# Gate and up of a decode block with stationary weights, and shorter norms

## The chip, the cores and the metric

The kernel runs on 1 core of one Trainium2 chip. The metric is device time in microseconds (us), as the median of several executions. The engines of the core that matter here are PE (TensorE: matmuls, and PEld, the loads of their stationary weights), DVE (VectorE), ACT (ScalarE), POOL (GpSimd) and SP (SyncE, whose queue issues all data transfers here). Each engine works through its own instructions in order; semaphores order them between engines.

## The reference, cut to what matters

```python
def _A_ref(x, k_cache, v_cache, wq, wo):
    q = (x @ wq).reshape(B, Sq, Hq, Dh).transpose(0, 2, 1, 3)
    k = jnp.repeat(k_cache, rep, axis=1)
    v = jnp.repeat(v_cache, rep, axis=1)
    scores = jnp.einsum("bhqd,bhkd->bhqk", q, k) * (Dh ** -0.5)
    o = jnp.einsum("bhqk,bhkd->bhqd", _softmax(scores), v)
    return o.transpose(0, 2, 1, 3).reshape(B, Sq, Hq * Dh) @ wo

def _B_ref(x, w_gate, w_up, w_down):
    h = _sigmoid(x @ w_gate) * (x @ w_up)
    return h @ w_down

x = x + _A_ref(_layernorm(x), A_k_cache, A_v_cache, A_wq, A_wo)
x = x + _B_ref(_layernorm(x), B_w_gate, B_w_up, B_w_down)
x = x + _A_ref(_layernorm(x), A_k_cache, A_v_cache, A_wq, A_wo)
x = x + _B_ref(_layernorm(x), B_w_gate, B_w_up, B_w_down)
```

Four batch rows, one token each, width 512, 32 query heads, 8 heads of keys and values with 4096 positions of 128 values, inner width 1792 (14 blocks of 128). All inputs are bfloat16. The two attention layers read the same caches.

## The kernel before, in words

One head of one batch row has 1 MB of keys and 1 MB of values. The kernel holds 12 slots of 1 MB each. `seq` lists all (layer, batch row, head) in the order worked out by hand in `ORDER`, which interleaves layer 1 of finished batch rows with layer 0 of the others; two heads make a group, 32 groups in all. Part of the slots (`RET`) are kept from layer 0 to layer 1, so that 52 MB of values and 48 MB of keys are loaded instead of 64 each.

The loop over `plan` (L1218) has 33 steps. Step k works on the softmax of group k (`sg`) and on the values of group k - 1 (`vg`), and prepares the keys of group k + 1 (`nxt`). In order, a step issues: the second scores of `sg` (L943), the sums of `vg` (L1017), `q_blocks` (POOL, L680), the first `k_turn` (a transpose of a slot on DVE, L928), `smax` (DVE, L966 and L970), one output projection `wo_pair` (L1130, with the addition to the residual x, L1144), `spread_max` (L977), `softmax` (L986 on DVE, L994 on ACT), `inverse` (L1027), the second `k_turn`, `pv` of the two heads (L1079), `normalise` (L1112), `ptrans` (L1039 on PE, 16 copies L1062 on ACT). The first scores of the next group come where `FIRST_AT` says. Since each engine keeps this order, whatever stands ahead of an instruction in its queue delays it.

`pump` (L383) issues the transfers in the fixed order of `loads`, built from the table `LOADS` (L327 to L363): it issues as long as a slot is free. A slot comes free when the scores that read the keys, or the pv that reads the values, are done; the queue on SP waits for that.

Between the two layers each batch row goes through a pass: norm, gate and up, down, norm, q. It is cut into 19 steps (`pass_steps`, L894), and `PLACES` (L57) says for every one at which point (0 to 8) of which loop step it is issued, relative to the step that ends the row's layer 0. The four passes run, by the profile, at about 92 to 114 us (row 0), 148 to 171 us (row 1), 205 to 229 us (row 2) and 262 to 285 us (row 3).

A pass works as follows. `ln_a` (L502): a matmul with ones sums x (L508), DVE takes the sum (L513), subtracts the mean (L520, float32 `xc`), ACT copies this to bfloat16 (`xc_bf`, L528), DVE squares it (L533). `ln_b_sum` sums the squares on PE (L585); `ln_b_rs` takes the sum (L593), divides and adds eps (L600), makes a first guess of the reciprocal root by integer arithmetic (L605) and refines it in three Newton steps of two instructions (L542, L550). The norm's factor `rs` is not applied to the operand but to what comes out of the matmuls. `gate_row` (L737) holds one column of `xc_bf` as weights and moves gate's weights, 512 or 384 columns at a time, 16 matmuls in all; each result is one row of PSUM, in four strips of partitions. `gate_tanh` (L754) makes half of rs (L756) and takes the tanh over 512 columns (L761). `up_row` (L766) is like gate. `up_gate` copies up's rows on ACT (L784) and multiplies on DVE (L786). `h_turn` turns the rows into 14 columns by 4 matmuls (L797) and copies them out (L803). `down` (L858) has stationary weights: 56 matmuls with a 128x128 block each and one moving column (L863). `down_add` adds to x in two instructions (L876, L886). Then come the second norm, `q_row`, `q_out`, `q_turn` and `q_spread`.

At the end all four rows go together through norm, `gate_up` (L690, stationary weights, four moving columns, L696) and `down_rows` (L1328), and the result leaves by one transfer.

Of the kernel before, what the change touches and what calls it, by code (L numbers as in the profile page):

```python
# [5 lines left out]
dt = mybir.dt  # L6
# [195 lines left out]
def bass_interleave_layers__gqa_block_cached__glu_gated_glu__decode_kernel(  # L202
# [17 lines left out]
    P = 128  # L220
# [12 lines left out]
    RSQRT_MAGIC = float(0x5F375A86)  # L233
    exp_scale = float(DH) ** -0.5
    RS = -1.0 / 8192.0
# [24 lines left out]
    rsg = small[:, 2:3]  # L260
# [14 lines left out]
    sq_sb = sbt([P, KD, Bn], dt.float32, "sq")  # L275
    dn_sb = sq_sb
    newt = sbt([P, 9, Bn], dt.float32, "newt")
    lnsum, lnsq, vpe, nt_a, nt_b, nt_c, nt_y, rs = [newt[:, i, :] for i in range(8)]
# [66 lines left out]
    need("k", 0)  # L345
    need("k", 1)
    for k, (_, vg) in enumerate(plan):
        sg = plan[k + 1][0] if k + 1 < len(plan) else None
        at = {"k": sg, "v": vg}
        got = {"k": 0, "v": 0}  # L350
        for o in range(2):
            for kind in LOADS[k][2 * o:2 * o + 2]:
                if at[kind] is not None:
                    need(kind, 2 * at[kind] + got[kind])
                got[kind] += 1
            if 2 <= 2 * k + o < 2 + HKV:
# [4 lines left out]
        assert got == {"k": 2, "v": 2}  # L361
# [140 lines left out]
    def ln_a(b0, nb):  # L502
# [15 lines left out]
        )  # L518
        dve(
            lambda e: e.scalar_tensor_tensor(  # L520
                out=xc_sb[:, :, 0:nb], in0=bc(lnsum[:, 0:nb], KD, nb), scalar=-inv_d, in1=xs,
                op0=ALU.mult, op1=ALU.add,
            ),
            reads=xkeys + ["lnsum"],
            writes=["xc"],
        )
        act(
            lambda e: e.activation(xc_bf[:, :, 0:nb], xc_sb[:, :, 0:nb], ACTF.Copy),  # L528
            reads=["xc"],
            writes=["xcb"],  # L530
        )
        dve(
            lambda e: e.tensor_tensor(sq_sb[:, :, 0:nb], xc_sb[:, :, 0:nb], xc_sb[:, :, 0:nb], ALU.mult),  # L533
# [4 lines left out]
    def newton_one(y0):  # L538
        y, yk = y0, "y0i"
        for it, three in enumerate((3.0, 12.0, 768.0)):  # L540
# [17 lines left out]
    def newton_many(y0, nb):  # L558
        y, yk = y0, "y0i"
        for it, three in enumerate((3.0, 12.0, 768.0)):  # L560
# [19 lines left out]

    def ln_b_sum(nb):
# [3 lines left out]
            lambda e: e.matmul(M[:, 32:32 + KD * nb], lhsT=ones_w, rhs=sq_sb[:, :, 0:nb], start=True, stop=True),  # L585
# [4 lines left out]
    def ln_b_rs(nb):  # L590
# [3 lines left out]
                lnsq[:, 0:nb], M[:, 32:32 + KD * nb].rearrange("p (k b) -> p b k", k=KD), AX.X, ALU.add  # L594
            ),
            reads=["M1"],
            writes=["lnsq"],
# [92 lines left out]
    def gate_up(nb, which, h=None):  # L690
# [14 lines left out]
        if which == 0:  # L705
# [11 lines left out]
                lambda e: e.activation(t_sb[:, 0:KF * nb], gs_sb[:, 0:KF * nb], ACTF.Tanh, scale=0.5 * RS),  # L717
# [689 lines left out]
```

## Time and profile before

| | us |
|---|---|
| median of 3 executions | 320.65 (319.68 to 321.61) |
| the profiled execution | 324.28 |
| its span, first to last instruction | 322.1 |
| PE busy, of the span | 221.3 |
| DVE busy | 183.6 |
| ACT busy | 139.6 |
| transfers (DMA): read from memory | 118.76 MB, 369 GB/s over the span |

The views used below: the page's first line and busy times; the chain of work that ended last; the busy time by stretch, whose columns are the stretch, its length, then for PE, PEld, DVE, ACT and POOL the busy time and (in brackets) the instructions, then PE's granted clock as a share, the share of the DMA engines and GB/s; the chain in order of time (start, duration, what); the timeline (start, duration, engine, line, operation, output<-inputs, shapes, how many; in square brackets the idle time ahead and what ended it); groups by line and shape (busy us, mean ns of one | idle time before and what ended it).

### The profile page before, as it was taken

The numbers are of one execution on the slowest core, as the hardware profiler recorded it, in microseconds if no ns is written. First come the engines' busy times: TensorE is split into PE (matmuls) and PEld (weight loads), VectorE is DVE, ScalarE is ACT, GpSimd is POOL, SyncE is SP. The second block draws the span as 40 slices with busy tenths as digits, with TensorE's granted clock in tenths as the row PEclk, the third lists the DMA queues.
The fourth block names the chain that finished last, engine by engine and source line by source line (L and its number), as shares of the span: only waits on it lengthen the run. The fifth ranks groups of instructions, "written<-read, shape, count | busy, mean of one in ns | idle before, by whom it ended". The sixth has DMA issues, their size and how long they took to land.

```text
span 322.1 us, 11493 instructions
## 1 busy us (share of the span) xinstructions
PE 221.3 (69%) x4892; PEld 154.8 (48%) x4892; DVE 183.6 (57%) x473; ACT 139.6 (43%) x602; POOL 25.8 (8%) x106
## 2 busy tenths in 40 slices
PE   1435413133278998868898787699885989988785
PEld 0423312122156565655656555555553665566675
DVE  4477343240656529965542898464776567469244
ACT  1005221204045257644615675452564753377530
POOL 0000000000000010110001001000100000020200
PEclk9999999999999555555755555575555555565555
DMA  7999999999999999998799999999999999999700
GB/s 293 428 422 408 403 404 402 401 387 388 401 415 367 360 382 424 419 419 326 245 368 355 425 422 418 419 388 378 371 421 421 421 418 404 391 371 424 322 3 5
DMA packets 22255, 119.50 MB, mean 371 GB/s; under 512 B 1976, under 2 KB 7868, under 8 KB 8892
## 3 DMA queue, kind: packets, MB, share of 16 engines
q1 hardware_dynamic: 22204, 118.77, 92.6%
q8 instruction: 39, 0.64, 0.8%
q14 instruction: 12, 0.10, 0.1%
HBM read 118.76 MB, written 0.00 MB: 369 GB/s over the span
## 4 chain that ended last, share of the span: by engine, by line
PE 33%; DMA 33%; DVE 16%; SPq 12%; issue 4%; ACT 1%; POOL 1%; DVEq 0%
DMA slot<-in_A_v_cache_dram 24%; PE O_ps L1079 9%; DVE slot L928 9%; PE S_ps L943 8%; SPq L403 6%; DMA wo<-in_A_wo_dram 5%; SPq L389 5%; PE M_ps L814 4%; DMA slot<-in_A_k_cache_dram 3%; PE O_ps L1130 3%; PE M_ps L508 2%; PE M_ps L863 2%; PE MS L977 2%; DVE small L966 1%; PE M_ps L696 1%
## 5 line engine op out<-in xcount | busy, mean ns | idle before, releaser
L1062 ACT ACTIVATE pT<-PT 32x64 bf16<-32x64 f32 x496 | 106.7, 215 | 67.1 <-PE PT L1039 54.1
L928 DVE STREAM_TRANSPOSE slot<-slot 128x2048 f32<-128x2048 f32 (+1 forms) x61 | 112.0, 1837 | 40.2 <-DMA slot<-in_A_k_cache_dram 40.2
L1079 PE MATMUL O_ps<-pT,slot 128*128 128x4 bf16 x1984 | 61.3, 167 | 29.4 <-DMA slot<-in_A_v_cache_dram 26.6
L1079 PEld LDWEIGHTS O_ps<-pT,slot 128*128 128x128 bf16 x1984 | 59.5, 104 | 36.1 <-DMA slot<-in_A_v_cache_dram 27.5
L943 PE MATMUL S_ps<-slot,qz 128*32 128x256 bf16 x1024 | 65.5, 409 | 14.7 <-DVE slot L928 11.2
L943 PEld LDWEIGHTS S_ps<-slot,qz 128*32 128x32 bf16 x1024 | 30.7, 128 | 32.1 <-DVE slot L928 13.0
L994 ACT ACTIVATE pe<-S_ps,small 128x256 bf16<-128x256 f32 x32 | 15.1, 473 | 50.0 <-issue 31.2
L1008 POOL TENSOR_TENSOR small<-small 128x1 f32<-128x1 f32 x64 | 12.4, 193 | 244.8 <-ACT pe L994 242.3
L977 PE MATMUL MS<-ident_bf,small 128*128 128x128 bf16 x64 | 12.5, 300 | 23.9 <-DVE small L970 23.6
L1130 PE MATMUL O_ps<-oT,wo 128*128 128x2 bf16 (+1 forms) x640 | 20.8, 165 | 4.9 <-issue 3.8
L1130 PEld LDWEIGHTS O_ps<-oT,wo 128*128 128x128 bf16 x640 | 19.1, 104 | 6.7 <-issue 4.6
L977 PEld LDWEIGHTS MS<-ident_bf,small 128*128 128x128 bf16 x64 | 4.2, 109 | 33.0 <-DVE small L970 26.3
L1112 DVE TENSOR_TENSOR oT<-O_ps,rden 128x8 bf16<-128x8 f32 x32 | 5.4, 168 | 24.9 <-PE O_ps L1079 24.7
L966 DVE TENSOR_REDUCE small<-S_ps 128x1 f32<-128x256 f32 x32 | 12.7, 397 | 12.0 <-PE S_ps L943 12.0
L680 POOL TENSOR_TENSOR qz<-qc,small 128x128 bf16<-128x128 bf16 x32 | 12.6, 399 | 35.4 <-ACT qc L666 35.4
L986 DVE CUSTOM_DVE_ANT_0 junk<-MS,mask_f,small 128x128 bf16<-128x128 f32 x32 | 10.7, 336 | 7.4 <-PE MS L977 7.2
L814 PE MATMUL M_ps<-wq,xc_bf 128*1 128x512 bf16 x128 | 14.5, 625 | 0.0
L1039 PE MATMUL PT<-ident_bf,pe 128*128 128x128 bf16 x64 | 11.7, 283 | 1.4 <-ACT pe L994 1.4
L666 ACT ACTIVATE qc<-M_ps 128x128 bf16<-128x128 f32 x8 | 1.9, 280 | 22.7 <-PE M_ps L655 22.7
L1017 PEld LDWEIGHTS MS<-head_b,small 128*128 128x128 bf16 x96 | 5.0, 107 | 12.7 <-issue 12.7
L1144 DVE TENSOR_TENSOR xT<-xT,O_ps 128x4 f32<-128x4 f32 x32 | 4.0, 157 | 12.0 <-PE O_ps L1130 11.8
L761 ACT ACTIVATE M_ps<-M_ps,small 128x512 f32<-128x512 f32 x4 | 2.6, 662 | 14.5 <-DVE small L756 14.5
(93 smaller groups left out, 171.9 us busy)
## 6 DMA issues: line engine op xcount, KB each, us to landing
slot<-in_A_v_cache_dram SPq DMA_DIRECT2D x52, 1024.0 KB, 11.4
slot<-in_A_k_cache_dram SPq DMA_DIRECT2D x48, 1024.0 KB, 10.8
wq<-in_A_wq_dram SPq DMA_DIRECT2D x4, 1024.0 KB, 7.6
wo<-in_A_wo_dram SPq DMA_DIRECT2D x8, 512.0 KB, 16.1
wg<-in_B_w_gate_dram SPq DMA_DIRECT2D x4, 448.0 KB, 13.8
wu<-in_B_w_up_dram SPq DMA_DIRECT2D x4, 448.0 KB, 14.2
wd<-in_B_w_down_dram SPq DMA_DIRECT2D x2, 896.0 KB, 16.5
row<-in_A_x_dram SPq DMA_DIRECT2D x1, 4.0 KB
```

Of the source, the lines that this page charges most:

```text
L389: S.dma("sp", (lambda dst, src: lambda e: e.dma_start(dst, src))(dst, src), f"wo{n}" if kind == "wo" else kind, writes=[f"{kind}{n}"])
L403: S.dma("sp", (lambda dst, src: lambda e: e.dma_start(dst, src))(dst, src), f"d{s}", writes=[f"s{s}"])
L680: lambda e: e.tensor_tensor(qz_sb[z][:, :, 0:4 * REP].rearrange("p i (a r) -> p i a r", r=REP), qc_sb[:, b, u:u + 2, :, :].rearrange("p u ...
L814: (lambda k, st: lambda e: e.matmul(M_ps[h][32 * st:32 * st + 1, :], lhsT=xc_bf[:, k, 0:1], rhs=wv[:, k, h, :, st, :], start=(k == 0), sto ...
L928: dve(lambda e: e.transpose(kf, kf), writes=[f"s{st}"])
L943: (lambda t, b2, e_, w0, s: lambda e: e.matmul(S_ps[p][32 * s:32 * s + 8 * REP, 0:2 * P], lhsT=qzf[:, w0:w0 + 8 * REP], rhs=ktv[:, :, s, : ...
L966: lambda e: e.tensor_reduce(m, S_ps[p][:, 0:2 * P], AX.X, ALU.max),
L977: (lambda n, col: lambda e: e.matmul(MS[:, 0:P], lhsT=top(col).broadcast_to([P, P]), rhs=ident_bf[:, :], start=(n == 0), stop=(n == 1)))(n ...
L994: lambda e: e.activation(pe_sb[p].rearrange("p j m -> p (j m)"), S_ps[p][:, 0:2 * P], ACTF.Exp, bias=nm_sb[p], scale=exp_scale, accum_out= ...
L1062: (lambda dst, frm: lambda e: e.activation(dst, frm, ACTF.Copy))(dst, frm),
L1079: (lambda x, c, j: lambda e: e.matmul(O_ps[p][:, ul * REP:(ul + 1) * REP], lhsT=vv[:, x * JG + c * 2 + j, :], rhs=pT[:, x, j, 2 * c + ul, ...
L1130: (lambda c, r: lambda e: e.matmul(O_ps[p][:, 64 + 2 * c:64 + 2 * c + nb], lhsT=wo_sb[:, u * REP + r, c * P:(c + 1) * P], rhs=oT_sb[n][:, ...
```

## The change

- `LOADS` is read in another way (one running count of keys and one of values, instead of counts within a step), with its first and last entries rewritten. A table `STEP` says for every step where the first `k_turn` stands, whether the first pv comes early, and whether the second `k_turn` is made in two halves; this last was a condition.
- In the passes gate and up become `wide`: 56 matmuls each, with a 128x128 block of the weights stationary and one moving column, into 14 columns of PSUM. `up_gate` and `h_turn` go; one DVE instruction, `gate_mul`, multiplies (tanh - 1) with up, straight into the columns that `down` reads. `PLACES` loses one entry for each row.
- In the norms DVE writes the bfloat16 operand itself, ahead of the float32 one. The squares get a fifth block that holds eps, so that the sum brings it along, and the division is folded into the constants of the Newton steps.
- A scale `RS` of -2 instead of -1/8192 saves the halving of rs. `down_add` is one instruction. The residual addition of a `wo_pair` with two rows is one instruction instead of two.

```diff
-    "kvkv", "kvkv", "kvkv", "vkkv", "kvkv", "kvkv", "kvkv", "vkvk",
+    "kkkk", "kvkv", "kvkv", "vkkv", "kvkv", "kvkv", "kvkv", "vkvk",
...
-    "vkkv", "kvkv", "kvkv", "kvkv", "kvkv", "kvkv", "kvkv", "kvkv",
-    "kvkv",
+    "vkkv", "kvkv", "kvkv", "kvkv", "kvkv", "kvkv", "kvkv", "vv",
+    "vv",
+)
+
+
+STEP = (
+    0, 0, 0, 0, 0, 0, 0, 6,
+    6, 6, 6, 6, 0, 6, 6, 6,
+    6, 6, 6, 0, 6, 6, 6, 6,
+    6, 6, 0, 0, 6, 6, 6, 0,
+    0,
 )
...
-    need("k", 0)
-    need("k", 1)
-    for k, (_, vg) in enumerate(plan):
-        sg = plan[k + 1][0] if k + 1 < len(plan) else None
-        at = {"k": sg, "v": vg}
-        got = {"k": 0, "v": 0}
+    got = {"k": 0, "v": 0}
+    for k, kinds in enumerate(LOADS):
         for o in range(2):
-            for kind in LOADS[k][2 * o:2 * o + 2]:
-                if at[kind] is not None:
-                    need(kind, 2 * at[kind] + got[kind])
+            for kind in (kinds[:2], kinds[2:])[o]:
+                need(kind, got[kind])
                 got[kind] += 1
...
-        act(
-            lambda e: e.activation(xc_bf[:, :, 0:nb], xc_sb[:, :, 0:nb], ACTF.Copy),
-            reads=["xc"],
-            writes=["xcb"],
-        )
+        for out, key in ((xc_bf, "xcb"), (xc_sb, "xc")):
+            dve(
+                (lambda out: lambda e: e.scalar_tensor_tensor(
+                    out=out[:, :, 0:nb], in0=bc(lnsum[:, 0:nb], KD, nb), scalar=-inv_d, in1=xs,
+                    op0=ALU.mult, op1=ALU.add,
+                ))(out),
+                reads=xkeys + ["lnsum"],
+                writes=[key],
+            )
...
-            lambda e: e.matmul(M[:, 32:32 + KD * nb], lhsT=ones_w, rhs=sq_sb[:, :, 0:nb], start=True, stop=True),
+            lambda e: e.matmul(M[:, 32:32 + (KD + 1) * nb], lhsT=ones_w, rhs=sq_sb[:, :, 0:nb], start=True, stop=True),
...
-        dve(
-            lambda e: e.tensor_scalar(vpe[:, 0:nb], lnsq[:, 0:nb], inv_d, eps, op0=ALU.mult, op1=ALU.add),
-            reads=["lnsq"],
             writes=["vpe"],
...
+    def wide(which):
+        wsb, keys = ((wg_sb, wkeys["wg"]), (wu_sb, wkeys["wu"]))[which]
+        fns = []
+        for fc in range(KF):
+            for k in range(KD):
+                fns.append(
+                    (lambda fc, k: lambda e: e.matmul(
+                        M_ps[which][:, 64 + fc:65 + fc],
+                        lhsT=wsb[:, k, fc * P:(fc + 1) * P],
+                        rhs=xc_bf[:, k, 0:1],
+                        start=(k == 0),
+                        stop=(k == KD - 1),
+                    ))(fc, k)
+                )
+        S.group("pe", fns, reads=["xcb"] + keys, writes=[f"M{which}"])
+
+    th = xc_sb.rearrange("p k b -> p (k b)")[:, 0:KF]
+
     def gate_tanh():
-        dve(
-            lambda e: e.tensor_scalar(rsg, rs[:, 0:1], 0.5 * RS, None, op0=ALU.mult),
-            reads=["rs"],
-            writes=["rsg"],
-        )
         act(
-            lambda e: e.activation(M_ps[0][:, :], M_ps[0][:, :], ACTF.Tanh, scale=rsg),
-            reads=["rsg"],
-            writes=["M0"],
-        )
+            lambda e: e.activation(th, M_ps[0][:, 64:64 + KF], ACTF.Tanh, scale=rs[:, 0:1]),
+            reads=["rs", "M0"],
+            writes=["xc"],
+        )
+
+    def gate_mul():
         dve(
             lambda e: e.scalar_tensor_tensor(
-                out=row_sb[:, :], in0=M_ps[0][:, :], scalar=1.0, in1=row_sb[:, :], op0=ALU.add, op1=ALU.mult
+                out=hT_bf[:, :, 0], in0=th, scalar=-1.0, in1=M_ps[1][:, 64:64 + KF], op0=ALU.add, op1=ALU.mult
             ),
...
         dve(
             lambda e: e.scalar_tensor_tensor(
-                out=xT[:, :, bsl(b0, nb)], in0=dn_sb[:, :, 0:nb], scalar=0.5 * RS, in1=xT[:, :, bsl(b0, nb)],
-                op0=ALU.mult, op1=ALU.add,
+                out=xT[:, :, b], in0=M_ps[0][:, 128:128 + KD], scalar=rs[:, 0:1], in1=xT[:, :, b],
+                op0=ALU.mult, op1=ALU.add,
             ),
...
-            gate_row,
+            lambda: wide(0),
             gate_tanh,
-            up_row,
-            up_gate,
-            h_turn,
+            lambda: wide(1),
+            gate_mul,
...
-        halves = k >= 7 and sg is not None and nxt is not None and not any((k, w) in steps for w in range(2, 5))
+        halves = halves and sg is not None and nxt is not None
+        if pv_first and vg is not None:
+            pv(2 * vg)
+            pump()
```

More of the change, by code (lines that the diff above doesn't have):

```diff
@@ L274, in bass_interleave_layers__gqa_block_cached__glu_gated_glu__decode_kernel @@
     xc_sb = sbt([P, KD, Bn], dt.float32, "xc")
-    sq_sb = sbt([P, KD, Bn], dt.float32, "sq")
-    dn_sb = sq_sb
+    sq_sb = sbt([P, KD + 1, Bn], dt.float32, "sq")
     newt = sbt([P, 9, Bn], dt.float32, "newt")
-    lnsum, lnsq, vpe, nt_a, nt_b, nt_c, nt_y, rs = [newt[:, i, :] for i in range(8)]
+    lnsum, _, vpe, nt_a, nt_b, nt_c, nt_y, rs = [newt[:, i, :] for i in range(8)]
     y0i = newt[:, 8, :].bitcast(dt.int32)
@@ L539, in newton_one @@
         y, yk = y0, "y0i"
-        for it, three in enumerate((3.0, 12.0, 768.0)):
+        for it, three in enumerate(RSQRT_STEPS):
             dve(
@@ L559, in newton_many @@
         y, yk = y0, "y0i"
-        for it, three in enumerate((3.0, 12.0, 768.0)):
+        for it, three in enumerate(RSQRT_STEPS):
             dve(
@@ L788, in up_gate @@
             ),
-            reads=["M0"],
-            writes=["row0"],
-        )
-    def h_turn():
-        fns = []
-        for j in range(4):
-            fns.append(
-                (lambda j: lambda e: e.matmul(
-                    M_ps[0][:, 4 * j:4 * j + 4], lhsT=row_sb[:, j * P:(j + 1) * P], rhs=strips, start=True, stop=True
-                ))(j)
-            )
-        S.group("pe", fns, reads=["row0"] + IDENT, writes=["M0"])
-        dve(
-            lambda e: e.tensor_copy(hT_bf[:, :, 0], M_ps[0][:, 0:KF]),
-            reads=["M0"],
+            reads=["xc", "M1"],
@@ L1250, in bass_interleave_layers__gqa_block_cached__glu_gated_glu__decode_kernel, with first_turn @@
         do_steps(k, 0)
-        if nxt is not None:
-            k_turn(2 * nxt)
-            pump()
+        turn_at, pv_first, halves = STEP[k] % 3, STEP[k] // 3 % 2, STEP[k] // 6
+        def first_turn(at):
+            if nxt is not None and turn_at == at:
+                k_turn(2 * nxt)
+                pump()
+        first_turn(0)
         do_steps(k, 1)
@@ L1272, in bass_interleave_layers__gqa_block_cached__glu_gated_glu__decode_kernel @@
         do_steps(k, 4)
-        if vg is not None:
+        if vg is not None and not pv_first:
             pv(2 * vg)
```

108 lines of the change are left out of this document (28 added, 80 removed), and 20 rows, old and new, of the table PLACES.

## The prediction

> **What bounds the kernel now.** I read first the page (span, engines, the chain that ended last), then the busy time by stretch, with edges set at the four passes, then the chain in order of time.
>
> ```profile
> span 322.1 us, 11493 instructions
> PE 221.3 (69%) x4892; PEld 154.8 (48%) x4892; DVE 183.6 (57%) x473; ACT 139.6 (43%) x602; POOL 25.8 (8%) x106
> PE 33%; DMA 33%; DVE 16%; SPq 12%; issue 4%; ACT 1%; POOL 1%; DVEq 0%
> 92.00:120.00 28.00, 25.43 (x497) 16.75 (x497) 14.33 (x52) 13.33 (x55) 2.00 (x9) 0.71 0.97 376
> 120.00:144.00 24.00, 18.18 (x436) 13.35 (x433) 22.03 (x38) 16.04 (x72) 2.84 (x13) 0.50 1.01 420
> 144.00:176.00 32.00, 28.74 (x572) 18.61 (x568) 14.46 (x55) 14.49 (x60) 2.37 (x11) 0.55 0.89 323
> 212.00:233.00 21.00, 18.62 (x396) 12.19 (x395) 12.82 (x34) 10.32 (x43) 2.08 (x9) 0.58 0.99 374
> 262.00:288.00 26.00, 23.13 (x441) 14.53 (x441) 16.22 (x53) 13.66 (x57) 1.56 (x7) 0.57 0.98 390
> 248.53 11.23 DMA slot<-in_A_v_cache_dram
> 259.81 1.02 PE O_ps L1079 x32
> ```
>
> The last figure of a stretch is the transfer rate in GB/s. Outside the passes the queue runs at 420, and time there cannot be won by faster computing. In the stretches with a pass it falls to 376, 323, 374 and 390: against 420 that is 28 x (1 - 376/420) = 2.9 us, 7.4 us, 2.3 us and 1.9 us in which the queue had too little to do, because matmuls freed the slots late. From 259.81 on the chain holds no transfer: the fourth pass and everything behind it is a chain of computing. So a pass step that comes earlier is worth its whole shift in pass 4, and up to the lost transfer time in passes 1 to 3.
>
> **What is no change.** Counted through, the new LOADS lists the same 118 loads in the same order as the old one, and STEP divided by 6 repeats the old condition for `halves` (with turn_at and pv_first 0 everywhere). PLACES loses the entry of `h_turn` alone. Order, slots and transfers stay; what moves is inside the passes.
>
> **The passes, worked on the fourth.**
>
> ```profile
> 263.37 0.17 DVE L520 SCALAR_TENSOR_TENSOR xc<-newt,xT 128x4 f32<-128x4 f32 x1
> 264.98 0.21 ACT L528 ACTIVATE xc_bf<-xc 128x4 bf16<-128x4 f32 x1
> 265.25 1.87 PE L744 MATMUL M_ps<-wg,xc_bf 128*1 128x512 bf16 x16 [0.54 <-ACT xc_bf L528]
> 266.30 0.16 DVE L970 TENSOR_TENSOR small<-small 128x1 f32<-128x1 f32 x1
> 267.05 0.39 PE L977 MATMUL MS<-ident_bf,small 128*128 128x128 bf16 x2
> 268.28 0.15 DVE L756 TENSOR_SCALAR small<-newt 128x1 f32<-128x1 f32 x1
> 268.80 2.26 DVE L928 STREAM_TRANSPOSE slot<-slot 128x2048 f32<-128x2048 f32 x1
> 270.98 0.65 DVE L786 SCALAR_TENSOR_TENSOR row<-M_ps,row 128x512 bf16<-128x512 f32 x1
> 271.78 0.25 PE L797 MATMUL M_ps<-ident_bf,row 128*128 128x4 bf16 x4 [0.74 <-DVE oT L1112]
> 272.06 0.19 DVE L803 CAST qT<-M_ps 128x14 bf16<-128x14 f32 x1 [0.35 <-PE M_ps L797]
> 272.31 1.65 PE L863 MATMUL M_ps<-qT,wd 128*128 128x1 bf16 x56
> L863 PE MATMUL M_ps<-qT,wd 128*128 128x1 bf16 x224 | 6.4, 164 | 0.9 <-DVE qT L803 0.9
> L723 DVE SCALAR_TENSOR_TENSOR slot<-pe,M_ps 128x56 bf16<-128x56 f32 x1 | 0.4, 402 | 0.4 <-ACT pe L717 0.4
> ```
>
> *Gate and up.* The nearest row for 56 matmuls with 128x128 weights and one moving column is `down`, L863: 224 in 6.4 us, 28.6 ns each, so 1.6 us for gate and 1.6 us for up, where the row form takes 1.87 us (L744, and L773 the same for up). On PE that is 0.27 us less, twice.
>
> The Trainium skill, "TensorE: Matmul & The Clock Gate", section "LDWEIGHTS (loading the stationary operand)", prices a load at its columns over 1.2 per ns, 107 ns for 128, and would speak against the change: 112 loads a pass would be 12.0 us by it. The trace disagrees as soon as loads follow each other: L863 sets 28.6 ns against it.
>
> *Operand of the norm.* The bfloat16 copy leaves ACT, where it waited behind 16 copies (it ran at 264.98 although xc was there at 263.54), and becomes a second VectorE instruction of L520's kind: 0.17 us and 0.03 us to the next, so +0.20 us on VectorE. Gate then starts at the end of the sum matmul, about 264.6 instead of 265.25. Queued behind the new instruction on VectorE is the first transpose of the step, then smax and with it spread_max (L977) on PE: that one is late next, and it moves from 267.05, where gate had held it, only to about 266.75, because smax's second instruction (L970) now ends at 266.46 + 0.20 us. Up follows it, so pv begins some 0.5 us earlier.
>
> *Small operations.* L756 (0.12 us to the next start, that of L986 at 268.40) and L600, of the same form (0.15 us and a gap of 0.04), go from VectorE: 0.20 - 0.19 - 0.12 = -0.11 us at the transpose that began at 268.80. Its end, 271.06, becomes 270.95. Then stood L786 (0.65), the turn on PE (L797) and its copy (L803), and `down` began at 272.31. Now one multiplication with 14 columns stands there. No row has it; L803 moves 14 columns out of PSUM in 0.19 us, L723 does this very operation on 56 columns in 0.40 us; these are the bounds, and I take 0.20 us, the shorter being nearest in columns. `down` starts 0.06 us behind it as it did behind L803: about 271.2, a gain of 1.1 us (0.9 with 0.40 us). The tanh over 14 instead of 512 columns and the dropped copy L784 lie on ACT beside VectorE; the cover is the transpose.
>
> In passes 2 and 3 the same steps stand at the same distances:
>
> ```profile
> 155.34 0.95 PE L1079 MATMUL O_ps<-pT,slot 128*128 128x4 bf16 x32 [0.29 <-DMA slot<-in_A_v_cache_dram]
> 156.40 0.65 DVE L786 SCALAR_TENSOR_TENSOR row<-M_ps,row 128x512 bf16<-128x512 f32 x1
> 157.65 1.62 PE L863 MATMUL M_ps<-qT,wd 128*128 128x1 bf16 x56 [0.28 <-DVE qT L803]
> 214.00 0.65 DVE L786 SCALAR_TENSOR_TENSOR row<-M_ps,row 128x512 bf16<-128x512 f32 x1
> 215.25 1.60 PE L863 MATMUL M_ps<-qT,wd 128*128 128x1 bf16 x56 [0.28 <-DVE qT L803]
> 101.55 0.27 PE L1039 MATMUL PT<-ident_bf,pe 128*128 128x128 bf16 x2
> 102.19 1.57 PE L863 MATMUL M_ps<-qT,wd 128*128 128x1 bf16 x56 [0.29 <-DVE qT L803]
> 103.99 0.17 DVE L886 SCALAR_TENSOR_TENSOR xT<-sq,xT 128x4 f32<-128x4 f32 x1
> ```
>
> From L786 to `down` are 1.25 us in both; 1.1 us go. Bounds of what is worth of it: 0 (the second pv of pass 2 waits for a transfer at 155.34, and nothing ahead of it gains) and 1.1. The slots freed behind `down` are the late ones, so I take 0.9 us for each. In pass 1 `down` can follow the transposes of ptrans directly, 101.82 instead of 102.19, since these wait for a pv that a transfer releases; and the one-instruction `down_add` saves L886's 0.19 us, which only there lies on PE's path (later passes put 16 score matmuls between): 0.5 us. The second norm of each pass gains nothing, PE is filled by scores and the q rows.
>
> *Tail* (304.00 to the end): the second VectorE instruction ahead of the squares is +0.20 us on the chain, the merged residual addition -0.06 us, L600 is hidden by the 112 gate and up matmuls: +0.1 us.
>
> Sum without the next term: -0.5 - 0.9 - 0.9 - 1.1 + 0.1 = -3.3 us.
>
> **PE's program grows.** 36 matmuls a pass become 112, each with its load: 152 more instructions a pass, 608 in all.
>
> ```profile
> q8 instruction: 39, 0.64, 0.8%
> PE O_ps L1130 <- issue: 3.8, 5, 1.3
> PE O_ps L1079 <- issue: 2.5, 4, 0.9
> 147.09 0.61 PE L1130 MATMUL O_ps<-oT,wo 128*128 128x1 bf16 x17 [0.56 <-issue]
> 292.49 1.55 PE L1079 MATMUL O_ps<-pT,slot 128*128 128x4 bf16 x53 [0.24 <-issue]
> 298.45 1.79 PE L1079 MATMUL O_ps<-pT,slot 128*128 128x4 bf16 x62 [0.93 <-issue]
> 304.48 0.27 PE L1130 MATMUL O_ps<-oT,wo 128*128 128x2 bf16 x4 [1.26 <-issue]
> 292.49:298.45 5.96, 5.03 (x127) 3.94 (x126) 5.21 (x14) 4.43 (x20) 0.74 (x3) 0.50 1.00 421
> 298.45:304.48 6.03, 4.77 (x128) 3.71 (x127) 0.75 (x3) 3.76 (x18) 2.18 (x8) 0.50 0.91 380
> ```
>
> 39 packets of instructions for 9784 matmuls and loads are one per 251. Nine times (waits for "issue": how long in all, how often, longest) PE stalls inside groups that wait for nothing, and from one stall to the next it runs 253 or 255 instructions and a few waits: a block of 256. So 9 of some 38 block ends stall, 0.24 to 1.26 us, all of them in dense matmuls, where by my count of the program about as many more ends lie that do not. The 608 instructions move every later block end to another place in the program. The four stalls quoted (the first delays pass 2; 2.99 us together) vanish from their places; by counting, eight other block ends come to lie in the starved stretches: two in pass 2, one in pass 3, two in pass 4, three behind it. At half of them with the mean of the four, 0.75 us, they cost 3.0 us: balance 0. Bounds: none stalls, -3.0; all stall as the longest, 8 x 1.26 - 3.0 = +7.1. I take -0.2, since those behind pass 4 now fall behind whole pv groups that begin with a wait. By the Trainium skill, "Runtime: NRT & Kernel Launch", section "Instruction fetch mechanics", blocks hold 256 instructions and crossing one is "mostly hidden"; by that this term is 0 in both kernels, and the sum -3.3. The size of the block agrees with the rows, the hiding does not.
>
> **Sum.** -3.5 us against the profiled execution, 324.28 us with a span of 322.1. The median of the runs, 320.65, is 1.1% below it; scaled, -3.5 us stay: 317.1 us.
>
> **Rivals.**
> *The gain of passes 1 to 3 is hidden anyway.* For it: the second pv of pass 2 waits for a transfer, and 420 GB/s cap everything. Against: 2.9, 7.4 and 2.3 us of lost transfers are more than the shift. Then only -1.1 + 0.1 - 0.2 remain: 319.5 us.
> *Slower: the block ends.* The eight stall at 1.1 us: 8.8 - 3.0 = +5.8, with -3.3 that is +2.5: 323.1 us. It decides (over +1.6 us) from (3.3 + 3.0 + 1.6) / 8 = 1.0 us each. For it: two of the four quoted are near 1; gate and up are now the densest code. Against: half of such ends show no stall.
> *Faster: none of the eight stalls.* -3.3 - 3.0 = -6.3, less half a microsecond for transfers that then arrive last: 314.9 us.
> *Loads are paid singly.* 112 at 0.164 us (the mean duration of one in L863's row) are 18.4 us, less 2 x 1.87 us +14.6 us a pass, four times: 379 us. That needs matmuls and loads that do not overlap, and L863 shows that they do.
> The Trainium skill's price of a load in "TensorE: Matmul & The Clock Gate" leads to this case, with +33 us.
>
> **How the numbers follow.** Forecast 0.58, hidden 0.17, slower by block ends 0.10, faster still 0.13, single loads 0.02. Half a per cent, 1.6 us, is what a measurement of this kernel tells from no change. Faster: 0.58 + 0.13 = 0.71; same 0.17; slower 0.12. The range 314.7 to 321.0 holds the forecast, the hidden and the faster case and leaves out the two slow ones.
>
> **What would show it.** Right: 56 gate matmuls in about 1.6 us; no ACT instruction between the norm and gate; `down` starting about 0.3 us behind the end of the second transpose in passes 2 to 4, not 1.25; rates above 323 and 374 GB/s in the stretches of passes 2 and 3; "issue" gaps at other lines than L1130 and L1079's first matmuls behind pass 4. Wrong: gate at 3 us or more; the rates unchanged; "issue" gaps that sum to 5 us or more from 150 us on; `down` still waiting for VectorE by a microsecond.

## The result, and the profile after

The changed kernel takes 319.55 us (median of 22 executions, 317.76 to 320.88). The kernel before took 321.90 us in its 22 executions taken alongside (319.68 to 323.29). The ratio is 0.9918, with a 95% interval of 0.9901 to 0.9935: about 2.6 us less. The forecast was 3.5 us less.

First the page of the changed kernel (span; busy time of the engines), then its busy time by stretch, with the columns that the prediction explains, then its waits of PE (engine, line, what it waited for, us in all, times, the longest).

```profile
span 317.6 us, 12066 instructions
PE 217.4 (68%) x5196; PEld 162.1 (51%) x5196; DVE 178.6 (56%) x449; ACT 133.7 (42%) x588; POOL 25.8 (8%) x106
```

```profile
92.00:120.00 28.00, 24.22 (x549) 17.69 (x550) 13.23 (x48) 11.65 (x51) 1.52 (x6) 1.00 0.96 365
120.00:144.00 24.00, 18.59 (x456) 13.83 (x453) 21.28 (x38) 15.77 (x73) 2.94 (x12) 1.00 1.00 414
144.00:176.00 32.00, 28.87 (x685) 21.47 (x685) 15.57 (x53) 14.59 (x64) 3.00 (x12) 0.88 0.93 361
212.00:233.00 21.00, 18.54 (x376) 11.94 (x376) 12.06 (x32) 9.88 (x43) 1.88 (x7) 0.50 1.01 413
262.00:288.00 26.00, 21.42 (x500) 15.41 (x497) 14.11 (x45) 11.32 (x49) 2.26 (x9) 0.57 0.96 375
```

```profile
PE O_ps L1022 <- issue: 3.4, 3, 2.3
PE M_ps L818 <- issue: 2.7, 2, 1.5
PE S_ps L886 <- issue: 1.3, 2, 1.0
```

PE has 304 more matmuls, DVE and ACT have fewer instructions, as counted. The transfer rate rose in the stretches of passes 2 and 3 (323 to 361, 374 to 413 GB/s) and fell in those of passes 1 and 4. The waits for "issue" are still there, 7.4 us as against 6.3 by these rows (7.51 and 6.24 with each stop added up), but at other lines: `down` (L818) and scores (L886) besides pv (L1022), no longer the output projection.

The steps of the passes, from the timeline of the changed kernel (start, us, what; in square brackets PE's idle time ahead and its cause). Norm of pass 1; the transpose, `gate_mul` and the start of `down` in pass 2; gate and up of pass 3:

```profile
92.81 0.17 DVE L520 SCALAR_TENSOR_TENSOR xc_bf<-newt,xT 128x4 bf16<-128x4 f32 x1
92.89 0.16 DVE L520 SCALAR_TENSOR_TENSOR xc<-newt,xT 128x4 f32<-128x4 f32 x1
93.08 0.17 DVE L528 TENSOR_TENSOR sq<-xc 128x4 f32<-128x4 f32 x1
...
154.06 2.26 DVE L871 STREAM_TRANSPOSE slot<-slot 128x2048 f32<-128x2048 f32 x1
156.24 0.15 DVE L756 SCALAR_TENSOR_TENSOR qT<-xc,M_ps 128x14 bf16<-128x14 f32 x1
156.51 0.64 PE L818 MATMUL M_ps<-qT,wd 128*128 128x1 bf16 x17
...
204.27 1.63 PE L735 MATMUL M_ps<-xc_bf,wg 128*128 128x1 bf16 x56
206.49 1.68 PE L735 MATMUL M_ps<-xc_bf,wu 128*128 128x1 bf16 x56
```

The 56 matmuls of gate and up take 1.63 and 1.68 us (forecast 1.6), `gate_mul` 0.15 us (forecast 0.20). The bfloat16 operand costs VectorE 0.08 us, the distance of its start to that of the float32 one, not 0.20. Now the places where PE stops inside `down` of passes 1 and 3, and pass 4 from its transpose on:

```profile
101.62 0.53 PE L818 MATMUL M_ps<-qT,wd 128*128 128x1 bf16 x13
103.39 1.30 PE L818 MATMUL M_ps<-qT,wd 128*128 128x1 bf16 x43 [1.24 <-issue]
...
210.61 0.53 PE L818 MATMUL M_ps<-qT,wd 128*128 128x1 bf16 x13
212.63 1.30 PE L818 MATMUL M_ps<-qT,wd 128*128 128x1 bf16 x43 [1.49 <-issue]
...
264.25 0.35 PE L1022 MATMUL O_ps<-pT,slot 128*128 128x4 bf16 x8
264.44 2.26 DVE L871 STREAM_TRANSPOSE slot<-slot 128x2048 f32<-128x2048 f32 x1
266.62 0.15 DVE L756 SCALAR_TENSOR_TENSOR qT<-xc,M_ps 128x14 bf16<-128x14 f32 x1
266.87 1.63 PE L1022 MATMUL O_ps<-pT,slot 128*128 128x4 bf16 x56 [2.27 <-issue]
268.53 1.68 PE L818 MATMUL M_ps<-qT,wd 128*128 128x1 bf16 x56
272.22 0.40 PE L886 MATMUL S_ps<-slot,qz 128*32 128x256 bf16 x2 [1.04 <-issue]
```

In pass 4 the product that `down` needs is there at 266.77, but pv, which stands ahead of `down` on PE, had stopped after 8 matmuls for 2.27 us, so `down` begins at 268.53. A second stop of 1.04 us follows in the scores. The step from the norm to the end of pass 4 is therefore read from `smax` to `smax` (the DVE instruction of steps 25 and 27), before and after:

```profile
256.29 0.39 DVE L966 TENSOR_REDUCE small<-S_ps 128x1 f32<-128x256 f32 x1
...
278.87 0.42 DVE L966 TENSOR_REDUCE small<-S_ps 128x1 f32<-128x256 f32 x1
```

```profile
252.45 0.38 DVE L909 TENSOR_REDUCE small<-S_ps 128x1 f32<-128x256 f32 x1
...
276.36 0.42 DVE L909 TENSOR_REDUCE small<-S_ps 128x1 f32<-128x256 f32 x1
```

Pass 4 took 22.6 us before and takes 23.9 us now. The stretch that was to win 1.1 us has lost 1.3. So in this pair of profiles the gain lies elsewhere, and the experiments look for it.

### The profile page after: what moved, and what is told of

The parts are those of the page before. It is cut to its first block, busy times and chain, and to the rows that moved or that the text cites. A ratio compares the mean times of both kernels' runs of the same rounds, so it can differ in the third digit from the quotient of the medians.

```text
span 317.6 us, 12066 instructions
## 1 busy us (share of the span) xinstructions
PE 217.4 (68%) x5196; PEld 162.1 (51%) x5196; DVE 178.6 (56%) x449; ACT 133.7 (42%) x588; POOL 25.8 (8%) x106
## 3 DMA queue, kind: packets, MB, share of 16 engines
q1 hardware_dynamic: 22204, 118.77, 93.4%
## 5 line engine op out<-in xcount | busy, mean ns | idle before, releaser
L1022 PE MATMUL O_ps<-pT,slot 128*128 128x4 bf16 x1984 | 61.4, 167 | 30.9 <-DMA slot<-in_A_v_cache_dram 26.9
L886 PE MATMUL S_ps<-slot,qz 128*32 128x256 bf16 x1024 | 65.7, 411 | 17.9 <-DVE slot L871 12.0
L1022 PEld LDWEIGHTS O_ps<-pT,slot 128*128 128x128 bf16 x1984 | 59.4, 105 | 34.8 <-DMA slot<-in_A_v_cache_dram 27.7
L886 PEld LDWEIGHTS S_ps<-slot,qz 128*32 128x32 bf16 x1024 | 30.5, 129 | 35.2 <-DVE slot L871 13.9
L1073 PE MATMUL O_ps<-oT,wo 128*128 128x2 bf16 (+1 forms) x640 | 20.1, 165 | 1.2 <-DVE oT L1055 0.7
L769 PE MATMUL M_ps<-wq,xc_bf 128*1 128x512 bf16 x128 | 13.7, 595 | 0.0
L818 PE MATMUL M_ps<-qT,wd 128*128 128x1 bf16 x224 | 7.0, 166 | 2.7 <-issue 2.7
L818 PEld LDWEIGHTS M_ps<-qT,wd 128*128 128x128 bf16 x224 | 6.8, 105 | 2.9 <-issue 2.9
```

The costliest lines, as they stand in the source:

```text
L769: (lambda k, st: lambda e: e.matmul(M_ps[h][32 * st:32 * st + 1, :], lhsT=xc_bf[:, k, 0:1], rhs=wv[:, k, h, :, st, :], start=(k == 0), sto ...
L818: (lambda c, k: lambda e: e.matmul(M_ps[0][:, 128 + c * nb:128 + (c + 1) * nb], lhsT=wd_sb[:, k, c * P:(c + 1) * P], rhs=hT_bf[:, k, 0:nb] ...
L886: (lambda t, b2, e_, w0, s: lambda e: e.matmul(S_ps[p][32 * s:32 * s + 8 * REP, 0:2 * P], lhsT=qzf[:, w0:w0 + 8 * REP], rhs=ktv[:, :, s, : ...
L1022: (lambda x, c, j: lambda e: e.matmul(O_ps[p][:, ul * REP:(ul + 1) * REP], lhsT=vv[:, x * JG + c * 2 + j, :], rhs=pT[:, x, j, 2 * c + ul, ...
L1073: (lambda c, r: lambda e: e.matmul(O_ps[p][:, 64 + 2 * c:64 + 2 * c + nb], lhsT=wo_sb[:, u * REP + r, c * P:(c + 1) * P], rhs=oT_sb[n][:, ...
```

## The experiments

In the traces every stop of PE for "issue" of over 0.12 us comes at the same point of its stream of instructions, once in 256 (a matmul and its load of weights counted as two, the waits counted too). I call this point a boundary. With each boundary goes one packet of 16 KB on the queue of instructions, which starts some time behind the boundary before. From the trace of the changed kernel, and below it from that with halved loads (e7):

```
        boundary  next refill packet   first instruction    stop there
        passed    starts               of the next block
after   247.88    251.74 (+3.86)       254.25 (+2.51)       0.23
        254.25    257.93 (+3.68)       260.31 (+2.38)       0.15
        260.31    264.32 (+4.00)       266.87 (+2.56)       2.27
        266.87    269.68 (+2.81)       272.22 (+2.54)       1.04
        307.77    308.25 (+0.48)       313.23 (+4.98)       none
e7      242.01    242.43 (+0.42)       246.56 (+4.13)       none
```

Wherever PE stopped, the packet had started 2.2 to 2.7 us earlier: that is the shortest way from packet to instruction. The packet itself starts 2.8 to 4 us behind the boundary passed in the first four rows, which lie ahead of and in pass 4, and 0.4 to 0.5 us behind it in the last two, where the loads are done (after, 3 GB/s from 306 to 312 us) or thin (e7, 138 GB/s from 240 to 247 us). In the first four rows a block of 256 instructions so lasts 5.4 to 6.6 us.

**Shifting the boundaries.** Theory: the stops in the passes took back about 3 us of the gain, and go if the boundaries lie elsewhere. Idle matmuls of one column were put on PE, with nothing else changed, in steps where it waits for other things:

```diff
+    PADS = {(3, 'm'): 72, (10, 'm'): 56, (18, 'p'): 56, (23, 'm'): 56}
+    def pad(k, at):
+        n = PADS.get((k, at), 0)
+        S.group("pe", [
+            lambda e: e.matmul((MS if at == "m" else PT)[:, 300:301], lhsT=ident_bf[:, :], rhs=ident_bf[:, 0:1], start=True, stop=True)
+        ] * n)
...
+        pad(k, "m")
         if sg is not None:
             spread_max(sg)
...
+            pad(k, "p")
             pv(2 * vg + 1)
```

That is e1; e2 has {(3, 'm'): 128} and e4 {(3, 'm'): 64} in the changed kernel, e3 has {(23, 'm'): 48} in the kernel before.

> The changed kernel plus 240 idle matmuls on TensorE (one column each, nothing reads them) in four waits of steps 3, 10, 18 and 23, so that in every pass a 256-instruction boundary of TensorE's stream lies some 23 instructions behind the start of gate's 56 matmuls, as it does in pass 2, which shows no stall. Theory (the stalls behind those boundaries took back 3 us of the gain): the stalls of 1.24, 0.79, 1.49, 2.27 and 1.04 us in the passes are gone or below 0.4 us each, and the time is 315 to 316.5 us against 319.5 for the changed kernel. Rival (boundaries cost nothing, the loads cap passes 1 to 3): 319.5 us within 0.7, whatever the gaps do.

> The changed kernel plus 128 idle matmuls (256 instructions) in one wait of step 3: a whole block, so that every boundary stays where it was in the program. Both theories: the stalls of the changed kernel stay at the same instructions with about the same lengths (1.24, 1.49, 2.27 and 1.04 us the longest), and the time is 319.5 us within 0.7; if idle matmuls themselves helped or hurt, it would show here.

> The changed kernel plus 64 idle matmuls (128 instructions, half a block) in one wait of step 3, so that every later boundary falls half a block earlier in the work. Theory: other stalls than in the changed kernel, at other lines, and a time that differs from 319.5 by the difference of the sums of the stalls in starved stretches (1 to 4 us, either sign). Rival (boundaries cost nothing): 319.5 within 0.7.

> The kernel before plus 48 idle matmuls (96 instructions) in the wait of step 23, ahead of pass 4: from there on every boundary falls 96 instructions earlier in the work, and the stalls of 0.24, 0.93 and 1.26 us in the final section should move off it. Theory: if they vanish without new ones in pass 4, 2.4 us less than before, 319.5; with new ones in pass 4 as many us more as the trace shows there. Rival (boundaries cost nothing): the time of before within 0.5.

Measured: e1 320.26 us, ratio to the kernel before 0.9932 (0.9897 to 0.9966); e2 320.04 us, 0.9931 (0.9903 to 0.9959); e4 320.88 us, 0.9954 (0.9927 to 0.9982); e3 319.65 us, 0.9942 (0.9919 to 0.9966). e1 missed the 315 to 316.5 us of the theory. The stops inside `down` of passes 1 and 3 are gone, but its timeline shows pass 4 stopped as long as ever, in pv:

```profile
265.66 0.78 PE L1022 MATMUL O_ps<-pT,slot 128*128 128x4 bf16 x24
269.00 1.21 PE L1022 MATMUL O_ps<-pT,slot 128*128 128x4 bf16 x40 [2.56 <-issue]
```

All its stops together are 7.65 us, against 7.51 in the changed kernel. Others came in their place, 1.39 and 1.10 us between 137 and 144 us among them. So a stop is not a matter of one unlucky place; another boundary can stop in its stead while the loads run. In e2, where the boundaries behind the idle matmuls stay where they were in the program, the stops of pass 3 and pass 4 came back (1.63 and 1.99 us), that of pass 1 did not, and the time lies in the 0.7 us allowed. e4 missed: its stops lie elsewhere, as expected, and sum to 5.59 us, 1.9 less than in the changed kernel, yet its median is 1.3 us higher (the profiled execution, 319.34 us, lies 1.5 us below that median). e3 came out near the theory: 48 idle matmuls make the kernel *before* 1.9 us faster by the ratio, although a new stop of 1.02 us came up in pass 4. The waits of PE in e3:

```profile
PE O_ps L1079 <- issue: 1.9, 3, 1.0
PE S_ps L943 <- issue: 0.6, 2, 0.4
PE O_ps L1130 <- issue: 0.2, 1, 0.2
```

Of the 2.43 us of stops in the final section only 0.18 us are left, and from the `smax` of step 27 to the end it takes 41.2 us instead of 43.2.

**Undoing the wide form.** In e5 gate and up go back to the row form in all passes, in e6 in pass 4 alone; norms and small operations stay as changed.

```diff
+    ROWS = (0, 1, 2, 3)
...
-            lambda: wide(0),
-            gate_tanh,
-            lambda: wide(1),
-            gate_mul,
+            *(
+                [gate_row, row_tanh, up_row, up_gate, h_turn]
+                if b0 in ROWS
+                else [lambda: wide(0), gate_tanh, lambda: wide(1), gate_mul]
+            ),
```

(`gate_row`, `up_row`, `up_gate` and `h_turn` as before, with the tanh scaled by `rs` and -1.0 in the product; `PLACES` of these rows as before; e6 has `ROWS = (3,)`.)

> The changed kernel with gate and up back in the row form of the kernel before in all four passes (16 matmuls each, the copy of up's rows, the product over 512 columns, the four matmuls that turn the rows, the copy of 14 columns); norms, bfloat16 operand and the small operations stay as changed. Theory one (the wide form gives the gain of the passes, as the prediction has it): 1.1 us are lost in each of passes 2 to 4, so about 322 us, the time of before. Theory two (while the loads run, TensorE gets a block of 256 instructions only about every 6 us, so the 608 added instructions cost about as much as the shorter chain on VectorE gains): within 1 us of the changed kernel, 318.5 to 320.5, with pass 4 (from the smax of step 25 to that of step 27, 24.0 us in the changed kernel, 22.6 before) at 22.5 or less.

> The changed kernel with the row form of gate and up in pass 4 alone. Theory one: pass 4 loses its 1.1 us, 320.6 against 319.5. Theory two: the 152 instructions that pass 4 no longer needs spare it the stalls of 2.27 and 1.04 us; the stretch from the smax of step 25 to that of step 27 falls from 24.0 to about 22.5 and the time to 318 to 319.

Measured: e5 321.82 us, ratio 1.0004 (0.9972 to 1.0037); e6 320.62 us, 0.9970 (0.9946 to 0.9995). Without the wide form nothing of the gain is left: at e5's positions of the boundaries the small operations and the bfloat16 operand on VectorE are worth nothing that can be measured. That speaks for theory one, and against theory two's 318 to 319 us for e6. What theory two said of pass 4 did happen: it took 22.4 us in e5 and 22.7 in e6, and its long stops were gone; the time did not follow. e6's time alone settles nothing, since e1, e2 and e4, with the passes unchanged, reach 320.0 to 320.9 us too. Nor does e5 alone: its boundaries lie nearly where those of the kernel before lie (PE stops at 140.44 and 146.89 us, before at 140.35 and 147.09), and e3 shows that moving them is worth 1.9 us in the row form.

**Loads of half the size.** In e7 (changed) and e8 (before) each load after the first 12 leaves out half of the columns, so the results use old keys and values there; the computing is the same.

```diff
             dst = slot[s][:, :]
+            count.append(n)
+            if len(count) > NSLOT:
+                dst, src = dst[:, 0:NJ * DH // 2], src[:, 0:NJ * DH // 2]
```

> The changed kernel, in which every load of keys or values after the first 12 moves half of the columns (512 KB in rows of 4 KB instead of 1 MB in rows of 8 KB); the other half of a slot keeps what it held. Theory two: the refill of TensorE's program waits behind the loads, so the time from a block boundary to the start of the next refill packet falls from 2.7 to 4.8 us to half or less, no stall in the passes is over 0.5 us, and the kernel is bound by computing alone: 290 to 305 us, 4 to 5 us below the kernel before with the same loads. Rival (the refill takes its time whatever the loads do): the wait for the packet stays at 2.7 us and more, and so do the stalls.

> The kernel before with the same halved loads, for comparison with the changed kernel with halved loads. Theory two: no stall over 0.5 us; the change is worth its whole local gain there, 4 to 5 us. If the gain of the wide form is hidden by something else than loads and refills, the two lie within 3 us.

Measured: 293.69 us changed, 301.33 us before: 7.6 us apart, more than either theory said. The mean time from a boundary to the next packet (between 100 and 262 us, some 25 blocks each) is 1.82 and 1.85 us; with whole loads it is 3.19 (after) and 3.31 us (before). So the refill waits less when there are fewer loads. The stops fall to 0.74 and 3.79 us; "no stall over 0.5 us" was missed in e8, which has one of 1.68 us at 186.85. The timelines of pass 4, kernel before with halved loads, then the changed one:

```profile
242.03 0.59 PE L513 MATMUL M_ps<-xT,small 128*128 128x4 f32 x2 [0.25 <-DVE xT L1149]
...
248.29 2.26 DVE L933 STREAM_TRANSPOSE slot<-slot 128x2048 f32<-128x2048 f32 x1
...
251.80 1.65 PE L868 MATMUL M_ps<-qT,wd 128*128 128x1 bf16 x56
...
256.76 0.15 DVE L605 TENSOR_SCALAR newt<-newt 128x1 f32<-128x1 f32 x1
...
258.36 0.42 DVE L971 TENSOR_REDUCE small<-S_ps 128x1 f32<-128x256 f32 x1
```

```profile
236.02 0.59 PE L512 MATMUL M_ps<-xT,small 128*128 128x4 f32 x2 [0.26 <-DVE xT L1093]
...
241.97 2.26 DVE L876 STREAM_TRANSPOSE slot<-slot 128x2048 f32<-128x2048 f32 x1
244.15 0.15 DVE L761 SCALAR_TENSOR_TENSOR qT<-xc,M_ps 128x14 bf16<-128x14 f32 x1
244.36 1.65 PE L823 MATMUL M_ps<-qT,wd 128*128 128x1 bf16 x56 [0.49 <-DVE oT L1060]
...
250.73 0.42 DVE L914 TENSOR_REDUCE small<-S_ps 128x1 f32<-128x256 f32 x1
```

Here, with no stop in the rows shown, the pass can be read by itself. From the norm's matmul to the transpose it takes 6.26 us before and 5.95 after (-0.31), to `down` 9.77 and 8.34 (-1.43), to the `smax` of step 27 16.33 and 14.71 (-1.62). That `smax` stands on VectorE behind the Newton steps of the second norm, where the division (L605 of this kernel, 0.19 us to the next start) is gone.

**Smaller transfers.** If a refill waits behind a number of packets, packets of half or a quarter of the size should shorten the wait. e9 issues every load of keys or values as two transfers, e10 as four:

```diff
-            S.dma("sp", (lambda dst, src: lambda e: e.dma_start(dst, src))(dst, src), f"d{s}", writes=[f"s{s}"])
+            step = NJ * DH // 2
+            S.group(
+                "sp",
+                [
+                    (lambda a, b: lambda e: e.dma_start(a, b))(dst[:, i:i + step], src[:, i:i + step])
+                    for i in range(0, NJ * DH, step)
+                ],
+                writes=[f"s{s}"], sem_key=f"d{s}", inc=16, needed=True,
+            )
```

> The changed kernel with every load of keys or values as two transfers of 512 KB with rows of 4 KB, the same bytes in the same order. Theory two (a refill of TensorE's program waits behind a number of packets of the loads): with packets of half the size the time from a block boundary to its refill packet falls from a mean of 3.2 us (100 to 262 us) towards the 1.8 us of the run with halved loads, the stalls sum to under 3 us instead of 7.5, and the time is 315 to 317.5 us. Rival (the wait goes by the bytes queued, or by how full the transfer engines are): wait and stalls stay, 319.5 us or more, as packets of 4 KB can only cost.

> The same with four transfers of 256 KB with rows of 2 KB. Theory two: a mean wait near 1 us, no stalls over 0.3 us, and 314 to 317 us, unless the rate of the loads falls below 420 GB/s with rows of 2 KB; then the time goes up with it. Rival: wait and stalls as in the changed kernel, 319.5 us or more.

Measured: 328.17 us, ratio 1.0178 (1.0125 to 1.0230), and 338.26 us, 1.0505 (1.0456 to 1.0555). The wait for the packet stayed (means of 3.29 and 3.28 us), and so did the stops (6.87 and 6.94 us). The rival holds: the wait does not go by the number of packets. Smaller ones only cost: by the row of transfers (queue: packets, MB, share of 16 engines over the span) the same bytes hold the engines for 96.8% of 338.4 us in e10, the first row, and for 93.4% of 317.6 us in the changed kernel, the second:

```profile
q1 hardware_dynamic: 65404, 118.79, 96.8%
```

```profile
q1 hardware_dynamic: 22204, 118.77, 93.4%
```

**The same kernels again.** How far is one profile to be trusted?

> The changed kernel itself, a second profile. If the stalls go by where the boundaries lie in the program alone, the same ones (1.24, 0.79, 1.49, 2.27, 1.04 us) stand at the same instructions; if they go by when each refill packet gets through the loads, lengths and places differ from profile to profile, with a sum near 7 us.

> The kernel before itself, a second profile: its sum of stalls was 6.24 us in an execution of 324.28 us, 2.4 us over its median. If the stalls make the spread of the runs, an execution near 322 us shows a sum near 4 us.

Measured: the changed kernel in an execution of 318.02 us, with stops of 5.15 us; the kernel before in one of 325.50 us, with 12.05 us. PE's timeline of the first, and PE's waits of the second:

```profile
265.54 1.64 PE L1022 MATMUL O_ps<-pT,slot 128*128 128x4 bf16 x56 [1.99 <-issue]
...
270.35 0.40 PE L886 MATMUL S_ps<-slot,qz 128*32 128x256 bf16 x2 [0.49 <-issue]
```

```profile
PE O_ps L1079 <- issue: 6.4, 5, 1.8
PE O_ps L1130 <- issue: 5.2, 4, 2.0
PE S_ps L943 <- issue: 0.4, 1, 0.4
```

Neither expectation fits alone. The stops of pass 3 (1.50 us) and pass 4 come back at the same instructions; that of 1.24 us in pass 1 is gone, and lengths vary. The spread between the two executions of the kernel before (322.1 and 323.5 us of span) is not the difference of their sums of stops (6.24 and 12.05 us). By the table below, 4.5 us more of stops in passes 1 to 3 cost 0.2 us, while behind step 27, where the prediction's chain holds no transfer any more, 1.4 us more cost as much. So in these two executions most stops of passes 1 to 3 cost nothing. No profile of the kernel before lies near its median, so the sum of 4 us is not tested.

**Where the time went, over all profiles.** From `smax` to `smax`, in us, with the stops in that stretch in brackets; each row is one execution. Steps 0 to 4 took 82.2 to 82.6 us wherever the loads were whole.

| kernel (form of gate and up) | steps 4 to 25: passes 1 to 3 | 25 to 27: pass 4 | 27 to the end |
|---|---|---|---|
| before (row) | 173.7 (3.8) | 22.6 (0.0) | 43.2 (2.4) |
| before again (row) | 173.9 (8.3) | 22.5 (0.0) | 44.7 (3.8) |
| e3 (row) | 170.3 (1.5) | 23.0 (1.0) | 41.2 (0.2) |
| e5 (row) | 169.5 (2.5) | 22.4 (0.3) | 44.1 (2.6) |
| changed (wide) | 170.1 (3.8) | 23.9 (3.7) | 41.2 (0.0) |
| changed again (wide) | 169.0 (2.0) | 23.1 (2.9) | 41.4 (0.3) |
| e1 (wide) | 171.8 (4.2) | 22.4 (3.0) | 41.7 (0.5) |
| e2 (wide) | 170.8 (3.9) | 22.8 (2.6) | 42.0 (0.5) |
| e4 (wide) | 169.3 (3.1) | 23.4 (1.7) | 42.3 (0.9) |
| e6 (wide, row in pass 4) | 171.3 (4.8) | 22.7 (0.5) | 42.0 (1.3) |
| e8, half loads (row) | 159.7 (1.8) | 22.5 (0.6) | 42.1 (1.4) |
| e7, half loads (wide) | 154.2 (0.7) | 20.1 (0.0) | 41.2 (0.0) |

Means of the first four rows in the row form and the five in the wide form: passes 1 to 3, 171.9 and 170.2 (-1.7); pass 4, 22.6 and 23.1 (+0.5); the rest 43.3 and 41.7 (-1.6). The sum is -2.7 us, close to the 2.6 us of the medians. The stops sum to 6.6 us a row in the row form and 6.8 in the wide form. Much hangs on single executions: "before again" took 325.50 us, longer than any of the 22 of the result, and without it the differences are -1.0, +0.5 and -1.1, -1.6 us together. And e3 is 3.4 us shorter than the first row in passes 1 to 3, although its idle matmuls stand only in step 23.

Two columns obey a simple rule. In the last one the time less its stops is 40.7 to 41.5 us in all kernels: every microsecond of stop counts there, and little else differs. In pass 4 it is 21.9 to 22.6 us in the row form (e6 and e8 included) and 20.2 us in three of the five wide rows and 20.1 in e7 (19.5 in e1, 21.7 in e4): the wide form is worth about 2 us in pass 4, and stops of 1.7 to 3.7 us take it back. In the first column the time less its stops is 166.2 to 167.6 us in the wide form (e6 included), but 165.6 to 169.9 in the row form with whole loads: there a stop may count or may not.

## Why the prediction came out right, point by point

The direction, the size within a microsecond and the range were right. That the wide form is the cause fits e5, where nothing of the gain is left, and the halved loads, where the change wins 7.6 us; with whole loads it is not shown, since positions of the boundaries alone move the time as much (below). And the sum was right in part by luck, because terms off in opposite directions met.

*Pass 4, -1.1 us.* The steps are as predicted, and the size was short. With halved loads `down` is 1.43 us earlier: 0.31 us of it at the transpose, where the prediction had 0.11 (mostly since the bfloat16 operand costs 0.08, not 0.20), and 1.12 behind it. Another 0.19 us comes from the second norm, of which the prediction said that it gains nothing: it saw PE filled by scores and q rows, and not that `smax` stands behind that norm on VectorE. Over the profiles the local gain is about 2 us. With whole loads it does not arrive: pass 4 got 0.5 us longer in the mean, and `down` begins 1.83 us behind the end of the transpose (266.70), not 0.3.

*Passes 1 to 3, -0.5, -0.9 and -0.9.* Together -2.3; measured -1.7 (-1.0 without "before again"), from executions that spread by 4.4 us in one form. With halved loads the same stretch wins 5.5 us, 4.4 without the stops. So more than half of the gain that computing alone gives does not arrive with whole loads, as the rival "hidden anyway" had it. The busy time from 92 to 262 us, in the changed kernel and with halved loads (the last two figures are the share of the transfer engines and GB/s):

```profile
92.00:262.00 170.00, 141.42 (x3309) 103.11 (x3310) 109.78 (x270) 89.54 (x397) 15.62 (x63) 0.72 0.99 398
```

```profile
92.00:262.00 170.00, 150.80 (x3534) 109.07 (x3535) 115.23 (x293) 96.73 (x426) 17.57 (x70) 0.70 0.65 220
```

With whole loads the transfer engines are full. The signs that the prediction named are there (rates up in passes 2 and 3, `down` 0.19 us behind the end of the transpose in pass 2, 156.51 against 156.32), yet `down` of pass 3 stops 1.49 us and that of pass 1 1.24 us. The prediction had a block end in pass 3, but priced it at half of 0.75 us, and none in pass 1. The rival's price, 319.5 us, is what was measured, but not by its sum: pass 4, which was to keep its 1.1 us, is the one that gained nothing.

*Tail, +0.1.* From step 27 to the end it is, without the stops, 41.0 us in the row form and 41.3 in the wide form, +0.3. The 1.6 us won there are stops that went (2.3 us a row before, 0.4 after).

*Block ends, -0.2.* The sum came out near by luck: all stops together are 6.6 us a row before and 6.8 after, though 6.24 and 7.51 us in the two first profiles. Of the eight ends that the prediction placed, the one in pass 3 and the two in pass 4 stopped, 1.49, 2.27 and 1.04 us: three, not four, but 4.80 us and not 3.0. The three behind pass 4 and the two in pass 2 did not stop, and a stop of 1.24 us in pass 1 was not foreseen. The sign that was to prove it wrong, stops of 5 us or more from 150 us on, did occur (5.97 us: 0.79, 1.49, 0.23, 0.15, 2.27, 1.04), without the loss that I had tied to it, for those of the final section went at the same time. What was mis-sized is the price of a stop, "at half of them" with 0.75 us, and what was missing is the cause: the refill packet starts some 3 us behind a boundary as long as the loads run and is 2.2 to 2.7 us on its way, and where PE is dense it uses up a block sooner than the next arrives. So a stop moved off one place can come back at the next: e1 has other places and the same sum. The sum is not fixed either: 2.65 us in e3, 12.05 in the second execution of the kernel before. By the Trainium skill, "Runtime: NRT & Kernel Launch", section "Instruction fetch mechanics", the next page is fetched while the current one runs, and crossing is "mostly hidden"; the packets agree with the first. With the second the stops do not agree while the loads are whole (7.5 us in the changed kernel), and with halved loads they do in e7 (0.7 us) but not in e8 (3.8 us).

*Slower by the block ends, from 1.0 us each.* Those of pass 4 reached that price. It did not decide, since the three ends behind pass 4 cost nothing and the old stops there vanished.

*Loads paid singly.* Refuted: 1.63 us for 56.

What stays open: how much of the 2.6 us belongs to the wide form as such. The kernel before with 48 idle matmuls is as fast as the changed kernel, 319.65 and 319.55 us, and the changed kernel with its boundaries shifted takes up to 320.88. Over the positions tried, the row form takes 321.9, 319.65 and 321.8 us, the wide form 319.55, 320.3, 320.0 and 320.9: a mean difference of 0.9 us, no more than positions alone can make. The executions speak against the granted clock as a rival, although it was 0.77 in the first profile of the changed kernel and 0.68 in that of the kernel before: among the 22 executions of the changed kernel the three at 0.86 took 319.1 to 320.5 us and the two near 0.69 took 319.9 and 320.4. No version tried beats the changed kernel.

## What to carry to other kernels

A faster form with many more instructions must be costed against the supply of instructions too: count the instructions of each dense stretch, and see in the trace how soon behind a boundary the refill packet starts while the loads run. Compare versions at several alignments (idle instructions where the engine waits anyway) before a difference of half a per cent is put down to an edit. And read the stretch that an edit touches by itself, between two fixed instructions: here pass 4 got slower, by 0.5 us in the mean of the profiles, while the whole got faster.

## What the runs showed of the hardware

- In all profiles, where PE stopped at a boundary, the refill packet had started 2.2 to 2.7 us before the first instruction of the new block. The packet starts on average 3.2 us behind the boundary before while the loads fill the engines, 1.8 us with halved loads, and 0.5 us in the row shown with the loads done.
- The wait does not shorten with rows of 4 KB or 2 KB in the loads (3.3 us); these make the changed kernel 2.6 and 5.9% slower (328.17 and 338.26 us).
- In the norm of pass 1 two VectorE instructions that do not depend on each other start 0.08 us apart (92.81 and 92.89), two that do 0.19 us (92.89 and the square at 93.08).
- PE's granted clock is 1.00 in the stretch 120 to 144 us after and 0.50 before, and gate takes the same 1.63 us in pass 1 (94.00 us, at 1.00) and in pass 3 (204.27 us, at 0.50). In the row form before it takes 1.87 us in pass 1 (94.83 us, at 1.00) and in pass 4 (265.25 us, at 0.50).
